# Moving a small VectorE operation behind a softmax, and three more edits to the first 20 microseconds of a fused convolution and two-layer product

## Chip, cores and metric

One core of a Trainium2 chip. The metric is the device time of one execution in microseconds (us). A run also has a span, the time from its first to its last instruction; here the time is the span plus about 1.7 us.

## The reference

```python
# x: (8, 4096, 192), weight: (8, 7), w_in: (192, 2048), w_out: (2048, 192)
w = exp(weight - max(weight)); w = w / (sum(w) + 1e-9)      # softmax over 7 taps, per head
y[b, s, h*24+d] = sum over k of w[h, k] * x_padded[b, s + k, h*24+d]   # causal, 7 taps
h = y @ w_in
g = maximum(0.01 * h, h)
out = g @ w_out                                             # (32768, 192), float32
```

## The kernel before

The sequence is cut into blocks of 512 positions of two batch rows; the first five are done as ten half blocks of 256, the rest whole. The 192 channels are three chunks of 64. For each block, VectorE (DVE) makes the seven taps of each chunk (`yt`), TensorE (PE) makes the main product with w_in into PSUM (`ph`), ScalarE (ACT) applies the leaky ReLU to it (`g`), and TensorE makes the output product with w_out (`po`). GpSimd (POOL) issues the loads of x, with a cast.

The first two half blocks (half 0 and half 1) differ: there TensorE itself makes the taps of two chunks of half 0 and of one chunk of half 1 (`acc`) with small diagonal weight matrices, each split into a high and a low bf16 part. These need a folded identity and the softmax:

```python
    load_w_in(0, 0)                                 # GpSimd: first piece of w_in
    ident = const_pool.tile([128, 128], BF16)
    make_identity(nc, ident)                        # GpSimd

    ident2 = const_pool.tile([128, CH], BF16)       # the fold, on VectorE
    nc.vector.tensor_add(ident2, ident[:, 0:CH], ident[:, CH:128])
    load_w_in(0, 1)                                 # second piece of w_in
    # ... further loads ...
    nc.vector.tensor_reduce(out=nmax, in_=w9[:, 0:K], ..., op=max, negate=True)   # softmax
    nc.scalar.activation(out=w9[:, 0:K], ..., func=Exp, bias=nmax, accum_out=...)
    # ... three bf16 parts w9p, VectorE ...
    warm(9); warm(1, 128)                           # TensorE on zeros, to raise its clock
    select(wps_hm, slice(0, 2)); warm(3); select(wps_l, 2); warm(7); warm(1, 128)
    nc.vector.tensor_copy(out=whm, in_=wps_hm)
    diag_high(0)                                    # VectorE
    cast_first(0, 0, nc.vector.tensor_copy)
    diag_low(0, range(2))                           # ScalarE
    cast_first(0, 1, nc.scalar.copy)
    transpose_first(0)
    warm(5)
    # ...
    diag_low(0, range(2, K)); diag_high(1); diag_low(1, range(K))
```

The taps on VectorE, of which the first has one tensor operand and the other six have two:

```python
                if k == 0:
                    jobs.append(lambda ...: nc.vector.tensor_scalar_mul(d, s, wk[:, c, 0:1]))
                else:
                    jobs.append(lambda ...: nc.vector.scalar_tensor_tensor(
                        out=d, in0=s, scalar=wk[:, c, k : k + 1], in1=d, op0=mult, op1=add))
```

And in the loop over groups, while the main product of the first half block runs (`u` counts its units of 12 matmuls):

```python
                if i == 0 and 2 <= u <= 5:          # half 1's taps of chunk 0 on TensorE
                    n = len(pe_ahead) // 4
                    for job in pe_ahead[(u - 2) * n : (u - 1) * n]:
                        job()
```

Of the kernel before, what the change touches and what calls it, by code (L numbers as in the profile page):

```python
# [10 lines left out]
BF16 = mybir.dt.bfloat16  # L11
# [3 lines left out]
def kernel(  # L15
# [8 lines left out]
    nc = tc.nc  # L24

    B, S, D = x.shape
    H, K = weight.shape
# [7 lines left out]
    CH = 64  # L35
# [13 lines left out]
    const_pool = ctx.enter_context(tc.tile_pool(name="const", bufs=1))  # L49
# [35 lines left out]
    def transpose_x(blk):  # L85

        if blk >= NBLK:
            return
        rp, st = divmod(blk, NB)
        if st == 0:  # L90
            new_xt(rp)
        t = x_bf.pop(blk)
        for c in range(NCH):
            nc.sync.dma_start_transpose(
                out=xt[rp][:, c, HALO + st * ST : HALO + (st + 1) * ST].rearrange(
                    "p (s k) -> p s k", s=SUB
                ),
                in_=t[:, c, :, :, :].rearrange("p s e k -> p (s e k)"),
            )
# [39 lines left out]
    def cast_first(q, e, copy):  # L139
        copy(  # L140
            out=x_half[q][:, :, :, e, :],
            in_=x_nat[q][:, e, :, :].rearrange("p s (c k) -> p c s k", c=NCH),
        )
# [3 lines left out]
    def transpose_first(q):  # L147
        ts = [
            psum_o.tile([128, HS, NCH, CH], BF16, name=f"ptr{i}", tag="po") for i in range(2)
        ]  # L150
        for s in range(HS):
            for c in range(NCH):
                for i in range(2):
                    ps = slice(i * CH, (i + 1) * CH)
                    if q != 2:
                        nc.tensor.transpose(  # L156
                            out=ts[i][:, s, c, :],
                            in_=x_half[q][ps, c, s, :, :].rearrange("p e k -> p (e k)"),
                            identity=ident[ps, ps],
                        )  # L160
                        continue
                    for e in range(2):
                        nc.tensor.transpose(  # L163
                            out=ts[i][e * CH : (e + 1) * CH, s, c, :],
                            in_=x_rows[ps, e, s, c * CH : (c + 1) * CH],
                            identity=ident[ps, ps],
                        )
        ptr[q] = ts

    def evac_first(q, *copies):  # L170
        dst = xt[0][:, :, HALO + q * HT : HALO + (q + 1) * HT].rearrange(
            "p c (i k s) -> p i s c k" if q == RUNS else "p c (s i k) -> p i s c k",
            s=HS, i=2,
        )
        for i, t in enumerate(ptr.pop(q)):
            copies[i](out=dst[:, i], in_=t)  # L176
# [4 lines left out]
    def conv_jobs(grp, chunks=range(NCH)):  # L181
        blk, t0, T = grp
        rp, st = divmod(blk, NB)
        if blk not in yt:
            yt[blk] = yt_pool.tile([128, NCH, ST], BF16, name="yt")
        y = yt[blk]
        jobs = []
        for c in chunks:
            for k in range(K):
                a = BASE + k + st * ST + t0  # L190
                src = xt[rp][:, c, a : a + T]
                dst = y[:, c, t0 : t0 + T]
                if k == 0:
                    jobs.append(
                        lambda s=src, d=dst, c=c: nc.vector.tensor_scalar_mul(  # L195
                            d, s, wk[:, c, 0:1]
                        )
                    )
                else:
                    jobs.append(  # L200
                        lambda s=src, d=dst, c=c, k=k: nc.vector.scalar_tensor_tensor(  # L201
                            out=d, in0=s, scalar=wk[:, c, k : k + 1], in1=d,
                            op0=mybir.AluOpType.mult, op1=mybir.AluOpType.add,
                        )
                    )
        return jobs
# [44 lines left out]
    def load_w_in(half, e):  # L251
        fs = slice(half * F // 2, (half + 1) * F // 2)
        nc.gpsimd.dma_start(  # L253
            out=w_in[half][e * CH : (e + 1) * CH],
            in_=moe_w_in[:, fs].rearrange("(c p) f -> p c f", p=CH),
        )

    load_w_in(0, 0)
    ident = const_pool.tile([128, 128], BF16)
    make_identity(nc, ident)  # L260

    ident2 = const_pool.tile([128, CH], BF16)
    nc.vector.tensor_add(ident2, ident[:, 0:CH], ident[:, CH:128])  # L263
    load_w_in(0, 1)
    for e in range(2):
        load_w_in(1, e)
# [14 lines left out]
    def warm(n, cols=HT):  # L281
        for _ in range(n):
            nc.tensor.matmul(  # L283
                out=wa[:, 0, 0:cols], lhsT=zero[:, 0:128], rhs=zero[:, 0:cols],
                start=True, stop=True,
            )
# [17 lines left out]
    nc.vector.tensor_sub(w9p[:, 1], w9, w9p[:, 0])  # L304
    nc.vector.tensor_sub(w9r, w9, w9p[:, 0])
    nc.vector.tensor_sub(w9p[:, 2], w9r, w9p[:, 1])
    warm(9)
    warm(1, 128)
    wps = psum_h.tile([128, 2, ST], FP32, name="wps", tag="ph")
# [17 lines left out]
    whm = const_pool.tile([128, NCH, 2, K + 1], FP32, name="whm")  # L327
# [2 lines left out]

    diag = [const_pool.tile([128, 2, K, CH], BF16, name=f"diag{c}") for c in range(NPEC)]

    def diag_high(c):
        nc.vector.tensor_mul(
            diag[c][:, 0],
            ident2[:, None, :].to_broadcast([128, K, CH]),
            whm[:, c, 0, 0:K, None].to_broadcast([128, K, CH]),
        )

    def diag_low(c, ks):  # L340
        for k in ks:
            nc.scalar.activation(  # L342
                out=diag[c][:, 1, k, :], in_=ident2,
                func=mybir.ActivationFunctionType.Copy, scale=whm[:, c, 1, k : k + 1],
            )

    diag_high(0)
    cast_first(0, 0, nc.vector.tensor_copy)
    diag_low(0, range(2))
    cast_first(0, 1, nc.scalar.copy)  # L350
    transpose_first(0)
    warm(5)
    wraw = const_pool.tile([128, NCH, K + 1], FP32, name="wraw")
    nc.vector.tensor_add(wraw, whm[:, :, 0], whm[:, :, 1])
    nc.vector.tensor_add(wraw, wps_l, wraw)
# [4 lines left out]
    nc.vector.tensor_mul(wk, wraw[:, :, 0:K], rsum.to_broadcast([128, NCH, K]))  # L360
    evac_first(0, nc.vector.tensor_copy, nc.scalar.copy)
    diag_low(0, range(2, K))
    diag_high(1)
    diag_low(1, range(K))

    def act_scale(out, in_, scale):
        nc.scalar.activation(  # L367
# [125 lines left out]
    for i, grp in enumerate(groups):  # L493
        blk, t0, T = grp
        steps = T // 64
        if t0 == 0:
            g[blk] = g_pool.tile([128, NFC, 2, ST], BF16, name="g", tag="g")
        quota = (avail - slot) // steps

        if i == 0:  # L500
            ahead = []
        else:
            ahead = conv_jobs(groups[i + 1]) if i + 1 < len(groups) else []
        per = -(-len(ahead) // steps)
        for j in range(steps):
            for u in range(2 * j, 2 * j + 2):
                mm1(grp, u)
                if i == 0 and u == 0:
                    transpose_first(1)
                    evac_first(1, nc.vector.tensor_copy, nc.vector.tensor_copy)  # L510
                    pe_ahead, evac_y = pe_conv_jobs(groups[1], 0)
                    ahead = conv_jobs(groups[1], range(1, NCH))
                    per = len(ahead)
                if i == 0 and 2 <= u <= 5:

                    n = len(pe_ahead) // 4
                    for job in pe_ahead[(u - 2) * n : (u - 1) * n]:
                        job()
                if i == 0 and u == 5:
                    evac_y(act_scale)  # L520
                if i == 0 and u == 6:
                    transpose_first(2)
            if i == 1 and j == 3:
                transpose_first(3)
            jobs = ahead[per * j : per * (j + 1)]
            if T == ST:


                jobs = ahead[len(ahead) * j // steps : len(ahead) * (j + 1) // steps]
                for job in jobs:  # L530
                    job()
                jobs = []
            for _ in range(quota):
                mm2_slot(slot)
                slot += 1
            if i == 0 and j == 3:
                evac_first(2, nc.vector.tensor_copy, nc.vector.tensor_copy)
            if i == 2 and j == 1:
                transpose_x(2)
            for job in jobs:  # L540
                job()
            if i == 1 and j == 3:
                evac_first(3, nc.vector.tensor_copy, nc.vector.tensor_copy)

            last_half = t0 + T == ST
            if j == steps // 4 and last_half:
                load_x(blk + 3)
            if j == steps // 2 and last_half and blk > 0:
                transpose_x(blk + 2)
        avail += 2 * T // 128 * NFC  # L550
# [36 lines left out]
```

## Time and profile before

| | before |
|---|---|
| time, first three runs | 694.65 us median (694.23 to 695.94) |
| span of the profiled run | 692.2 us |
| TensorE busy | 685.9 us, 99% |
| VectorE busy | 541.9 us, 78% |

The page gives busy times over the whole span and the chain of waits that ended last. The prediction below shows the lines that carried it. Instructions of before in order of time (start, length, engine, line, operation, output<-inputs, sizes, count):

```profile
113.35 4.69 DVE L201 SCALAR_TENSOR_TENSOR yt<-xt,wk,yt 128x512 bf16<-128x512 bf16 x6
...
117.71 1.49 PE L402 MATMUL ph<-yt,w_in 64*128 64x512 bf16 x12
```

VectorE's last six taps of the first whole block end at 118.04. TensorE starts that block's first product at 117.71 and, after two chunks of it, needs those taps near 118.1. Both engines arrive together; neither waits. From 14.20 to 118.04 VectorE has no idle time longer than 0.1 us.

### The profile page before, as it was taken

Reading aid. Unit: us, or ns where it says so; the run is one execution under the profiler, and the core shown is the slowest. Engines: PE = TensorE matmul, PEld = TensorE weight load, DVE = VectorE, ACT = ScalarE, POOL = GpSimd, SP = SyncE. Lnnn points to the kernel's source line nnn. Section 1 sums busy time; section 2 is a strip of 40 time slices with the busy share of each in tenths; the row PEclk is TensorE's granted clock in tenths of the full one; section 3 lists DMA queues with packets and bytes.
Section 4 is the critical chain, followed back from the end, with each engine's and each line's share of the span. In section 5 each row is a group of like instructions: output and inputs, shape, how many; then the busy total and the mean of one; then the engine's idle time right before and its main releaser. Section 6 shows DMA issues by size and latency. Waiting matters only on the chain.

```text
span 692.2 us, 26117 instructions
## 1 busy us (share of the span) xinstructions
PE 685.9 (99%) x11800; PEld 584.1 (84%) x11800; DVE 541.9 (78%) x1000; ACT 517.2 (75%) x578; POOL 144.6 (21%) x202
## 2 busy tenths in 40 slices
PE   8999999999999999999999999999999999999998
PEld 5899999788888888888888888888888888888887
DVE  5999998977878787878787878877878878787812
ACT  6888888977777777777777777777777777777771
POOL 5822211402222202222112222102222022000000
PEclk9999999999999999999999999999999999999999
DMA  9976635955565545566455565445665355322112
GB/s 175 106 90 82 92 66 78 82 82 75 66 93 81 71 78 73 71 89 86 65 78 74 78 82 85 74 75 70 83 81 79 74 74 67 70 60 59 48 42 65
DMA packets 183456, 54.00 MB, mean 78 GB/s; under 512 B 148528, under 2 KB 182576, under 8 KB 183344
## 3 DMA queue, kind: packets, MB, share of 16 engines
q0 software_dynamic: 98576, 14.56, 29.9%
q1 hardware_dynamic: 84768, 37.77, 23.6%
q8 instruction: 92, 1.51, 1.0%
q14 instruction: 20, 0.16, 0.1%
HBM read 29.88 MB, written 25.17 MB: 80 GB/s over the span
## 4 chain that ended last, share of the span: by engine, by line
PE 97%; ACT 2%; POOL 0%; DVE 0%; issue 0%; POOLq 0%
PE po L431 48%; PE ph L402 47%; ACT g L412 1%; PE acc L220 1%; PE warm L283 1%; POOL w_in L253 0%; POOL sel L242 0%; PE ptr L156 0%; PE wps L316 0%; ACT yt L367 0%; ACT w L295 0%; DVE o_sb L478 0%; PE ptr L163 0%; POOL ident masks.py:199 0%; POOL sel L240 0%
## 5 line engine op out<-in xcount | busy, mean ns | idle before, releaser
L412 ACT ACTIVATE g<-ph 128x1024 bf16<-128x1024 f32 x512 | 496.5, 1021 | 153.0 <-PE ph L402 152.6
L201 DVE SCALAR_TENSOR_TENSOR yt<-xt,wk,yt 128x512 bf16<-128x512 bf16 (+1 forms) x648 | 442.4, 683 | 17.7
L431 PEld LDWEIGHTS <-g 64*128 64x128 bf16 (+1 forms) x8064 | 360.6, 94 | 34.0 <-issue 0.2
L431 PE MATMUL po<-w_out,g 64*128 64x192 bf16 (+1 forms) x8064 | 387.3, 243 | 0.0
L402 PE MATMUL ph<-yt,w_in 64*128 64x512 bf16 (+1 forms) x3552 | 384.1, 347 | 1.2 <-ACT g L412 0.5
L402 PEld LDWEIGHTS <-w_in 64*128 64x128 bf16 x3552 | 227.3, 110 | 64.7 <-issue 4.1
L79 POOL DMA_DIRECT2D x_bf<-in_x_dram x180 | 133.9, 774 | 426.3 <-DMA xt<-x_bf 316.1
L478 DVE COPY o_sb<-po 128x192 f32<-128x192 f32 x216 | 77.1, 357 | 121.5 <-PE po L431 115.3
L195 DVE TENSOR_SCALAR yt<-xt,wk 128x512 bf16<-128x512 bf16 (+1 forms) x108 | 37.3, 345 | 1.5 <-DMA xt<-x_bf 1.4
L478 ACT COPY o_sb<-po 128x192 f32<-128x192 f32 x40 | 12.8, 321 | 2.1 <-PE po L431 0.2
L283 PE MATMUL warm<-zero 128*128 128x256 bf16 (+1 forms) x28 | 6.4, 399 | 1.1 <-DVE junk L237 1.1
L220 PE MATMUL acc<-xt,diag 64*64 64x256 bf16 x84 | 6.0, 274 | 0.0
L134 POOL DMA_DIRECT2D x_half<-in_x_dram x6 | 4.3, 716 | 6.5 <-DMA w_in<-in_moe_w_in_dram 6.5
L220 PEld LDWEIGHTS <-diag 64*64 64x64 bf16 x84 | 4.3, 107 | 1.5 <-issue 1.0
L283 PEld LDWEIGHTS <-zero 128*128 128x128 bf16 x28 | 3.4, 135 | 2.6 <-DVE junk L237 1.1
L342 ACT ACTIVATE diag<-ident,whm 128x64 bf16<-128x64 bf16 x14 | 3.6, 335 | 2.0 <-DVE whm L328 2.0
L176 DVE COPY xt<-ptr 128x384 bf16<-128x384 bf16 x7 | 2.6, 414 | 2.1 <-PE ptr L156 2.1
L253 POOL DMA_DIRECT2D w_in<-in_moe_w_in_dram x4 | 2.6, 665 | 0.0
L316 PEld LDWEIGHTS <-sel 8*64 8x64 bf16 x12 | 0.6, 139 | 1.7 <-issue 1.4
L367 ACT ACTIVATE yt<-acc,rsum 128x256 bf16<-128x256 f32 x3 | 1.4, 466 | 0.8 <-PE acc L220 0.8
L289 ACT ACT_TABLE_LOAD x1 | 1.3, 1283 | 0.8 <-PEq L571 0.8
L263 DVE TENSOR_TENSOR ident<-ident 128x64 bf16<-128x64 bf16 x1 | 0.2, 192 | 2.1 <-POOL ident masks.py:199 2.1
(37 smaller groups left out, 14.7 us busy)
## 6 DMA issues: line engine op xcount, KB each, us to landing
out_dram<-o_sb SPq DMA_DIRECT2D x118, 192.0 KB, 2.1
x_bf<-in_x_dram POOLq DMA_DIRECT2D x180, 64.0 KB, 3.3
out_dram<-o_sb SPq DMA_DIRECT2D x20, 96.0 KB, 1.6
w_in<-in_moe_w_in_dram POOLq DMA_DIRECT2D x4, 384.0 KB, 10.0
xt<-x_bf SPq DMA_TRANSPOSE x90, 2.5
w_out<-in_moe_w_out_dram POOLq DMA_DIRECT2D x1, 768.0 KB, 14.6
x_nat<-in_x_dram SPq DMA_DIRECT2D x2, 192.0 KB, 2.6
x_nat<-in_x_dram SPq DMA_DIRECT2D x1, 384.0 KB, 8.4
```

The source lines that it names most:

```text
L79: nc.gpsimd.dma_start(out=t[:, c, :, e, :], in_=src[2 * rp + e, :, :, c * CH : (c + 1) * CH],)
L134: nc.gpsimd.dma_start(out=x_half[q][:, c, :, e, :], in_=rows[:, e, :, c * CH : (c + 1) * CH],)
L176: copies[i](out=dst[:, i], in_=t)
L195: lambda s=src, d=dst, c=c: nc.vector.tensor_scalar_mul(d, s, wk[:, c, 0:1])
L201: lambda s=src, d=dst, c=c, k=k: nc.vector.scalar_tensor_tensor(out=d, in0=s, scalar=wk[:, c, k : k + 1], in1=d, op0=mybir.AluOpType.mult, ...
L220: lambda k=k, p=p, a=a, e=e, ps=ps: nc.tensor.matmul(out=acc[ps, :T], lhsT=diag[c][ps, p, k, :], rhs=xt[0][ps, c, a : a + T], start=(k == ...
L283: nc.tensor.matmul(out=wa[:, 0, 0:cols], lhsT=zero[:, 0:128], rhs=zero[:, 0:cols], start=True, stop=True,)
L342: nc.scalar.activation(out=diag[c][:, 1, k, :], in_=ident2, func=mybir.ActivationFunctionType.Copy, scale=whm[:, c, 1, k : k + 1],)
L402: nc.tensor.matmul(out=ph[:, e, i * T : (i + 1) * T], lhsT=w_in[f * 2 // NFC][ps, c, f // RUN % 2 * RUN * 128 + f % RUN : (f // RUN % 2 + ...
L412: act = nc.scalar.activation(out=g[blk][:, nf * u : nf * (u + 1), :, t0 : t0 + T], in_=ph.rearrange("p e (i t) -> p i e t", i=nf), func=my ...
L431: return nc.tensor.matmul(out=po[m], lhsT=g[b][ps, fc, e, s * 128 : (s + 1) * 128], rhs=w_out[ps, fc, :], start=start, stop=stop,)
L478: ins = copy(out=o_sb[:, n % 2, :], in_=po.pop(n))
```

## The change

Its intent is to shorten the start. The fold goes behind the softmax on VectorE, so that the softmax does not wait for GpSimd's identity. Three of the second tap set's seven low parts go from ScalarE to VectorE. Two warm-up matmuls go. Half 1's taps on TensorE come in two parts of 14 matmuls instead of four of 7.

```diff
     make_identity(nc, ident)
-
-    ident2 = const_pool.tile([128, CH], BF16)
-    nc.vector.tensor_add(ident2, ident[:, 0:CH], ident[:, CH:128])
     load_w_in(0, 1)
...
     nc.vector.tensor_sub(w9p[:, 2], w9r, w9p[:, 1])
+
+    ident2 = const_pool.tile([128, CH], BF16)
+    nc.vector.tensor_add(ident2, ident[:, 0:CH], ident[:, CH:128])
     warm(9)
...
-    def diag_high(c):
+    def diag_wide(c, p, n):
         nc.vector.tensor_mul(
-            diag[c][:, 0],
-            ident2[:, None, :].to_broadcast([128, K, CH]),
-            whm[:, c, 0, 0:K, None].to_broadcast([128, K, CH]),
+            diag[c][:, p, 0:n],
+            ident2[:, None, :].to_broadcast([128, n, CH]),
+            whm[:, c, p, 0:n, None].to_broadcast([128, n, CH]),
         )
...
-    diag_high(0)
+    diag_wide(0, 0, K)
...
-    warm(5)
+    warm(3)
...
-    diag_high(1)
-    diag_low(1, range(K))
+    diag_wide(1, 0, K)
+    diag_wide(1, 1, 3)
+    diag_low(1, range(3, K))
...
-                if i == 0 and 2 <= u <= 5:
+                if i == 0 and u in (2, 5):
 
-                    n = len(pe_ahead) // 4
-                    for job in pe_ahead[(u - 2) * n : (u - 1) * n]:
+                    n = len(pe_ahead) // 2
+                    for job in pe_ahead[(u - 2) // 3 * n : (u + 1) // 3 * n]:
                         job()
```

## The prediction

> **What bounds the kernel now.** I read the page first, then the chain of waits over the first 36 us, then the instructions in order of time over the first 30 us, and last the list of DMA completions that the trace keeps. Page:
>
> ```profile
> span 692.2 us, 26117 instructions
> PE 685.9 (99%) x11800; PEld 584.1 (84%) x11800; DVE 541.9 (78%) x1000; ACT 517.2 (75%) x578; POOL 144.6 (21%) x202
> PE   8999999999999999999999999999999999999998
> PE 97%; ACT 2%; POOL 0%; DVE 0%; issue 0%; POOLq 0%
> ```
>
> TensorE is on the path for 97% of the span. Going through the starts of its matmuls, I find only four steps longer than 0.45 us, and all lie before 24 us. Two things follow. The change touches only what is done before 24 us, so it can move the end only by what it saves there. And what it saves there reaches the end, because no later wait on a transfer is there to absorb it. The start of the chain of waits:
>
> ```profile
> 2.90 0.30 POOL ident masks.py:199
> 3.20 0.02 issue
> 3.23 0.19 DVE ident L263
> 3.42 0.07 DVE nmax L291
> ...
> 4.33 0.33 PE wps L316 x6
> 4.67 0.75 PE warm L283 x3
> 5.42 0.25 PE wps L316 x3
> 5.66 1.71 PE warm L283 x8
> 7.38 0.43 PE ptr L156 x12
> 7.81 1.18 PE warm L283 x5
> 8.99 1.74 PE acc L220 x24
> ...
> 12.75 0.48 ACT yt L367
> 13.23 0.04 issue
> 13.27 0.75 PE ph L402 x10
> ```
>
> Columns are start, length and what ran. The reader is to see that GpSimd's identity, through the small VectorE addition that folds it (L263), releases the maximum of the softmax (L291), and that everything up to 13.27 hangs on that: selection, transposes, tap products (acc), then ScalarE's scaling of the second tap product (yt). Only after that does the main product (ph) run past its first pair. In order of time:
>
> ```profile
> 3.23 0.19 DVE L263 TENSOR_TENSOR ident<-ident 128x64 bf16<-128x64 bf16 x1 [2.15 <-POOL ident masks.py:199]
> 3.33 0.14 DVE L291 TENSOR_REDUCE nmax<-w 8x1 f32<-8x7 f32 x1
> 8.25 2.97 ACT L342 ACTIVATE diag<-ident,whm 128x64 bf16<-128x64 bf16 x12
> 12.64 0.30 PE L402 MATMUL ph<-yt,w_in 64*128 64x256 bf16 x2
> 12.83 0.71 POOL L134 DMA_DIRECT2D x_half<-in_x_dram  x1 [1.73 <-DMA w_in<-in_moe_w_in_dram]
> ```
>
> The last line is the one that matters most: it is a bystander on GpSimd that waits for the second piece of w_in to land and goes at 12.83. The completions of that piece run from 9.67 to 12.54. The first main product needs this piece for its second matmul, and it went at 12.64. So the weights came in only 0.1 us before they were wanted.
>
> **What the Trainium skill says.** "TensorE: Matmul & The Clock Gate", Architectural detail: the array is 16× 32×32, says that VectorE and ScalarE queues are strict first in, first out. The trace agrees: the small weight's last completion is at 2.36, yet the reduction that needs nothing else starts at 3.33, right behind the addition. The same page, What's actually happening, says that TensorE runs at half clock until a busy window of about 3.4 us has passed, and that the window runs freely from run to run. The trace agrees: 256-column warm-up matmuls start 0.213 us apart up to 9.13, and pairs of tap matmuls of 256 columns 0.109 apart after it. "TensorEngine Tiling (Array Packing)", Key Properties, says that a change of tiling mode drains the array; here the weight loads stand still 0.20 us at each change between main product and tap product. "DMA: Bandwidth & Descriptors", Why a DMA increments its semaphore by 16 and not by 1, says only the full count means that all has landed; here the sixteenth completion comes 0.41 after the fifteenth (12.13, 12.54), so the slowest engine sets it.
>
> **The change part by part.**
>
> *The fold behind the softmax.* The reduction no longer waits for the identity. It can start at 2.36 plus the usual 0.04 of a released wait, 2.40 instead of 3.33: 0.92 us. Does someone else hold? ScalarE's first activation is over at 2.30, and the exponential would start at 2.59. TensorE's ten warm-ups let the first selection's weight load go at 3.26, and the selection would start at 4.33 − 0.92 = 3.41. So nearly all of 0.92 passes. The fold itself (0.19 us) moves into VectorE's idle 4.6 to 5.7 (now 3.7 to 4.8): free. Transposes: 7.31 → 6.39; their inputs' transfers completed at 3.79 and 4.35, so the casts move too.
>
> *Less warm-up.* Two matmuls of 0.213 go: 0.43 us. The first tap product goes from 8.92 to 8.92 − 0.92 − 0.43 = 7.57. Its input, ScalarE's copy, ends at 8.36 − 0.92 = 7.44: just in time. Sum so far 1.35.
>
> *Low parts on two engines.* Three of ScalarE's twelve scaled copies (0.238 apart) go: 0.71 us; ScalarE is free at 11.22 − 0.92 − 0.71 = 9.59. Without this it would be at 10.30, while the first tap product would end near 9.2, so it would start to hold the scaling. VectorE gets a multiplication of 192 columns; from the 448-column one (next instruction 0.53 later) I estimate 0.27. Its third-chunk taps end at 12.09 − 0.92 + 0.27 = 11.44, before they are wanted.
>
> *Where that sum goes.* Second tap product: complete at 12.72 now, then 12.72 − 1.35 = 11.37 if the clock is full by 7.57. If it turns full only at 9.13 as in this trace, 1.35 us more of taps run at half clock, which costs about 0.7: some 12.1. Scaling after it ends at 11.9 or 12.6. But the second piece of w_in comes at 12.54 whatever the compute engines do: GpSimd's issue order is untouched. So the first pair of the main product starts at about 12.60, the second at 12.71, instead of 13.27. Of 1.35 us only **0.56** is left; TensorE is expected to stand idle about a microsecond before 12.6.
>
> *Half 1's taps in two parts.* Now: four parts of 7 matmuls (3.5 pairs), each 0.55, each between main products of 0.78, hence 1.33 per unit. After: two parts of 14, each 7 × 0.109 + 0.11 = 0.87, so 0.46 less in all, and main products that follow another cost 0.655 instead of 0.78. Against that, with less TensorE work between them, units wait for ScalarE's 1.02 per unit. Counting from the start of the third unit: third 0 to 0.78, taps to 1.65, fourth to 2.31, fifth to 2.97; the sixth needs the bank that ScalarE frees at 3.54, so 3.58 to 4.36, taps to 5.24, seventh at 5.24. It is now at 20.45 − 15.12 = 5.33. Gain **0.09**; TensorE's saved work is mostly turned into one wait of 0.6.
>
> Sum on one clock phase: 0.56 + 0.09 = 0.65 us, 0.1% of the time.
>
> *The clock's phase.* Today TensorE has a hole of 1.0 us at 3.3 to 4.3, so a full busy window can begin only at 4.33 and the clock turns full, by the phase, somewhere in 7.7 to 11.2; every microsecond of that after 8.92 costs about half a microsecond. This would explain part of the spread of before (693.86 in the profiled run, 694.23 to 695.94 in the others). After, the hole shrinks to 0.15, so the clock should turn full up to 3.4 us sooner (5.7 on this trace's phase), and any remainder hides behind w_in. That is worth another 0 to 0.8 against the median.
>
> **The rivals.** (1) The whole 1.35 us shows, because w_in lands earlier than I think or the wait isn't binding: second pair at 11.9, time about 692.9. Against it: completion at 12.54 in the trace and a bystander that waited for it. (2) Nothing shows: w_in lands later than in this trace, since its slowest engine varies. 0.5 us later would eat the gain: 694.5. (3) The idle microsecond before the main product sends the clock back to half: up to 3.4 us at half speed costs 1.7, time about 695.3. Against it: today's hole of 1.0 us before 4.33 only delayed the rise, and I know no fall in this trace. (4) The two-part taps make ScalarE the bound: if its backlog is 0.3 longer than I count, the gain of 0.09 becomes a loss of 0.2, time about 693.8.
>
> **Range and chances.** 693.86 − 0.65 = 693.2 from the profiled run, 694.65 − 0.65 = 694.0 from the median; I take 693.6. The spread of before, 1.7 us, is larger than the effect, so the range is 692.5 to 694.9. Two per cent is 13.9 us, ten times all that the first 13 us could give; faster or slower by that much would need something quite unforeseen: within 2% at 0.98, 0.01 on each side.
>
> **What would show it.** Reduction at 2.4; first selection at 3.4; first tap product near 7.5; the main product's second matmul held until the second piece of w_in, near 12.6, with TensorE idle before it; the seventh unit 5.2 after the third; from there on starts earlier by 0.6 to 0.7 and unchanged steps of 2.63 per main product and output product. Full-clock spacing before 9 us would confirm the phase argument. If the main product starts before 12.3, the cap was wrong; if it starts at 12.6 and the end is still not earlier, something after 24 us absorbed it.

## The result, and the profile after

Ratios here and below are the mean time of one kernel's fast runs over that of the other's of the same rounds, so they are not quite the ratio of the medians quoted.

| | before | changed |
|---|---|---|
| time, first rounds (4 runs each) | 695.23 us median (694.23 to 695.94) | 693.18 us median (692.82 to 693.83) |
| ratio, first rounds | | 0.9973 (95%: 0.9955 to 0.9990) |
| ratio, later rounds (9 and 5 runs) | | 0.9986 (0.9973 to 0.9998) |
| span of the profiled run | 692.2 us | 692.1 us |

The change is 0.95 to 1.9 us faster by the mean, and within 2% by far. But the two profiled executions differ by only 0.1 us, so the traces say at once that something took a gain back in the one that was profiled. The start of the changed kernel, in order of time:

```profile
2.17 0.15 DVE L288 TENSOR_REDUCE nmax<-w 8x1 f32<-8x7 f32 x1 [1.10 <-DMA w<-in_weight_dram]
...
3.26 0.33 PE L316 MATMUL wps<-w9p,sel 8*64 8x16 bf16 x6
...
4.53 1.01 PE L280 MATMUL warm<-zero 128*128 128x256 bf16 x8
...
6.40 0.50 PE L280 MATMUL warm<-zero 128*128 128x256 bf16 x3
...
7.25 1.72 PE L220 MATMUL acc<-xt,diag 64*64 64x256 bf16 x28 [0.35 <-ACT diag L342]
...
11.68 0.84 PE L403 MATMUL ph<-yt,w_in 64*128 64x256 bf16 x11 [0.50 <-DMA w_in<-in_moe_w_in_dram]
...
12.71 1.06 DVE L176 COPY xt<-ptr 128x384 bf16<-128x384 bf16 x2 [1.40 <-PE ptr L156]
```

The reduction starts at 2.17 instead of 3.33, the tap product at 7.25 instead of 8.92, and the main product goes on at 11.68, when the second piece of w_in has landed, instead of 13.27. The eight warm-ups from 4.53 take 1.01 us where the same eight took 1.78 from 5.60 before: the clock turned full at 4.60 in the trace's clock record, against 9.13. VectorE starts its unbroken run of copies and taps at 12.71 instead of 14.20. So far 1.5 us are won. The place where half blocks give way to whole blocks, near 118 us: I call it **the switch**. The switch in the changed kernel:

```profile
113.33 4.69 DVE L201 SCALAR_TENSOR_TENSOR yt<-xt,wk,yt 128x512 bf16<-128x512 bf16 x6
...
116.18 0.63 PE L403 MATMUL ph<-yt,w_in 64*128 64x512 bf16 x4
...
118.08 1.06 PE L403 MATMUL ph<-yt,w_in 64*128 64x512 bf16 x8 [1.27 <-DVE yt L201]
```

TensorE comes at 116.18, 1.53 us earlier than before, and then stands still until 118.08 for VectorE. VectorE's last taps start at 113.33, against 113.35: it has lost all its lead. The page's chain of waits had turned accordingly:

```profile
PE 82%; DVE 14%; DMA 1%; ACT 1%; issue 1%; POOL 0%; POOLq 0%
```

VectorE was under 1% of this chain before, and TensorE 97%. Where did VectorE's lead go? All first taps of the two kernels from 12 to 119 us (duration in ns: least, median, longest), before and then changed:

```profile
L195 DVE TENSOR_SCALAR yt<-xt,wk x29: 280/281/349, 15.3 to 113.0; 128x256 bf16<-128x256 bf16 x26, 128x512 bf16<-128x512 bf16 x3
```

```profile
L195 DVE TENSOR_SCALAR yt<-xt,wk x30: 277/282/668, 13.8 to 118.5; 128x256 bf16<-128x256 bf16 x26, 128x512 bf16<-128x512 bf16 x4
```

The median is the same, but the longest went from 0.35 us, the ordinary length at 512 columns, to 0.67, at 256 columns. Six first taps of the changed kernel are stretched, by 1.47 us together; in before one is, by 0.02. An example from the changed kernel:

```profile
58.97 2.24 POOL L79 DMA_DIRECT2D x_bf<-in_x_dram  x3 [12.39 <-issue]
59.21 1.94 ACT L413 ACTIVATE g<-ph 128x1024 bf16<-128x1024 f32 x2 [0.29 <-PE ph L403]
59.21 0.53 DVE L195 TENSOR_SCALAR yt<-xt,wk 128x256 bf16<-128x256 bf16 x1
```

GpSimd had begun to issue a load of x at 58.97; the first tap began at 59.21, took 0.53 instead of 0.28, and the next tap could start only after it. The Trainium skill, "SBUF — State Buffer", Who interferes with whom, says that VectorE's one-tensor operations can use a port pair that is shared with GpSimd, and that whoever issues first holds it while the other blocks. The traces agree in part, as told at the end.

### The profile page after: what moved, and what is told of

Its sections match the earlier page's. It is cut to its first block, busy times and chain, and to the rows that moved or that the text cites. A ratio compares the mean times of both kernels' runs of the same rounds, so it can differ in the third digit from the quotient of the medians.

```text
span 692.1 us, 26111 instructions
## 1 busy us (share of the span) xinstructions
PE 684.0 (99%) x11798; PEld 584.3 (84%) x11798; DVE 543.6 (79%) x1001; ACT 516.6 (75%) x575; POOL 144.6 (21%) x202
## 4 chain that ended last, share of the span: by engine, by line
PE 82%; DVE 14%; DMA 1%; ACT 1%; issue 1%; POOL 0%; POOLq 0%
PE po L432 42%; PE ph L403 40%; DVE yt L201 13%; DMA w_in<-in_moe_w_in_dram 1%; DVE yt L195 1%; ACT g L413 1%; DVE xt L176 0%; POOL w_in L253 0%; POOL sel L242 0%; DVE o_sb L479 0%; POOL sel L240 0%; PE ptr L156 0%; POOL ident masks.py:199 0%; POOL ident masks.py:197 0%; POOLq masks.py:199 0%
## 5 line engine op out<-in xcount | busy, mean ns | idle before, releaser
L280 PE MATMUL warm<-zero 128*128 128x256 bf16 (+1 forms) x26 | 4.9, 340 | 1.1 <-DVE junk L237 1.1
L140 ACT CAST x_half<-x_nat 128x384 bf16<-128x384 f32 x3 | 1.5, 503 | 0.3 <-DMA x_nat<-in_x_dram 0.3
```

What stands on the lines that cost most here:

```text
L280: nc.tensor.matmul(out=wa[:, 0, 0:cols], lhsT=zero[:, 0:128], rhs=zero[:, 0:cols], start=True, stop=True,)
```

## The experiments

Three theories were set down before the runs. **V**: the gain of the start must pass through VectorE's unbroken chain of taps, which ends at the switch. **P**, the prediction's: TensorE alone sets the pace, and what it saves early reaches the end. **C**: the phase of TensorE's clock alone makes the difference. The expectation of the fourth run extended V by the stretching, and the sum below stood in that of the fifth, so before three of the seven traces in its table were taken.

**The account that all traces share.** In every trace in which VectorE neither idles before the switch nor has other work, three numbers read from the trace add up: the start of its chain (the first copy `xt<-ptr` of half 1), the stretching (first taps over 0.281 us at 256 columns or 0.347 at 512, summed), and the end of the taps of the first whole block.

| kernel | second w_in piece landed | chain starts | chain ends | length | stretch | length less stretch | span less end |
|---|---|---|---|---|---|---|---|
| before | 12.54 | 14.20 | 118.04 | 103.84 | 0.02 | 103.82 | 574.11 |
| changed | 11.63 | 12.71 | 118.03 | 105.32 | 1.47 | 103.85 | 574.06 |
| fold only | 12.12 | 13.20 | 118.47 | 105.27 | 1.44 | 103.83 | 574.04 |
| all but the fold | 12.21 | 14.16 | 119.20 | 105.04 | 1.23 | 103.81 | 574.07 |
| changed, again | 11.82 | 12.90 | 117.25 | 104.35 | 0.51 | 103.84 | 574.04 |
| more TensorE work | 11.92 | 13.00 | 118.15 | 105.15 | 1.33 | 103.82 | 574.05 |
| w_in first | 10.38 | 15.88 | 120.39 | 104.51 | 0.68 | 103.83 | 574.07 |

Chain start + 103.8 + stretch + 574.1 gives the span to 0.1 us in all seven. TensorE's saving in the first 24 us doesn't appear in it at all, except through the start of the chain. That start in turn follows the landing of w_in: in all nine traces with the fold behind the softmax and the old order of issue it comes 1.08 or 1.09 us after it.

### The fold alone

```diff
-    ident2 = const_pool.tile([128, CH], BF16)                          # before the softmax
-    nc.vector.tensor_add(ident2, ident[:, 0:CH], ident[:, CH:128])
...
     nc.vector.tensor_sub(w9p[:, 2], w9r, w9p[:, 1])
+    ident2 = const_pool.tile([128, CH], BF16)
+    nc.vector.tensor_add(ident2, ident[:, 0:CH], ident[:, CH:128])
```

> The kernel before with one part of the change alone: the fold of the identity moved behind the softmax. Theory V (the prologue's gain must pass through VectorE's unbroken chain of taps, which ends at the switch from half to whole blocks near 118 us, and is there as large as the lead that chain still has): reduction at 2.2 to 2.4, clock full before 6 us, VectorE's chain starts 0.9 to 1.5 us earlier than the 14.20 of before because w_in caps it, and the time is 0.5 to 2 us under before, ratio 0.997 to 0.9993, most of what the whole change gives. Theory P (the prediction's: the end moves by what TensorE saves before 24 us): 0.5 to 0.9 us under before. Theory C (the clock's phase alone makes the measured 2 us): the clock turns as early as in the changed kernel, so the ratio is that of the whole change, 0.997.

Measured: 694.23 us median (693.65 to 695.59), before in the same rounds 695.01; ratio 0.9993 (0.9979 to 1.0006), which the interval leaves unclear. By the means it is 0.53 us faster, at the lower edge of what V and P both expected. The trace is clearer:

```profile
6.43 0.72 PE L280 MATMUL warm<-zero 128*128 128x256 bf16 x5
...
7.23 1.72 PE L220 MATMUL acc<-xt,diag 64*64 64x256 bf16 x28
...
12.16 0.74 PE L402 MATMUL ph<-yt,w_in 64*128 64x256 bf16 x10 [1.00 <-DMA w_in<-in_moe_w_in_dram]
```

With five warm-ups and all low parts on ScalarE, the tap product starts at 7.23, as in the changed kernel at 7.25, and the main product waits for w_in just the same. In the trace the fold is thus the whole gain of the start; the rest of the change shortens nothing that is waited for. The profiled run lost 1.44 us to stretching. Theory C as I wrote it expected 0.997 here, which lies outside the interval, by a little; the whole change's later ratio, 0.9986, lies inside, so this doesn't settle C.

### All of it but the fold

```diff
     make_identity(nc, ident)
+    ident2 = const_pool.tile([128, CH], BF16)
+    nc.vector.tensor_add(ident2, ident[:, 0:CH], ident[:, CH:128])
...
-    ident2 = const_pool.tile([128, CH], BF16)                          # behind the softmax
-    nc.vector.tensor_add(ident2, ident[:, 0:CH], ident[:, CH:128])
```

> The changed kernel with the fold put back in front of the softmax, all other parts kept. Reduction again near 3.3, TensorE's hole of 1 us back. Theory V and P: first tap product 0.43 us earlier than before (two warm-ups less), main product some 0.3 to 0.5 us earlier, time 0.2 to 0.6 us under before. Theory C: clock turns as late as before, so the time is that of before, ratio 1.000 within 0.0007.

Measured: 694.87 us median (694.11 to 695.95), ratio 1.0000 (0.9985 to 1.0015). The tap product started 0.44 earlier (8.48), but the clock was not yet full, and it took 2.20 instead of 1.81:

```profile
8.48 2.20 PE L220 MATMUL acc<-xt,diag 64*64 64x256 bf16 x28
```

So the two warm-ups taken away came back as slower taps, and the chain started at 14.16. My expectation of 0.2 to 0.6 us (V and P) was missed by the mean, though the interval, 1 us to each side, would allow it; the trace shows its error, which was to count warm-ups as pure cost while the clock was still half. Theory C's number, 1.000, was met. This run therefore doesn't tell C from V as the table has it: in both the late clock leaves the start where it was. What speaks against C as the whole cause is that the clock enters the table only through the start of the chain, and that the stretching, all of it seen while the clock was full, moves the span as much.

### Relieving VectorE with ScalarE, first try, on the changed kernel and on before

```diff
-                if k == 0:
+                if k == 0 and c == 2 and 0 < blk < NHALF:
+                    jobs.insert(0, lambda ...: nc.scalar.activation(
+                        out=d, in_=s, func=Copy, scale=wk[:, c, 0:1]))
+                elif k == 0:
```

> The changed kernel, with the first tap of the third chunk of the eight half blocks from 2 to 9 made on ScalarE instead of VectorE: 2.5 us less work in VectorE's chain up to the switch near 118 us, 8 times some 0.4 us more on ScalarE, TensorE's work unchanged. Theory V: TensorE's wait of 1.3 us for VectorE at the switch is gone, the switch comes 1 to 1.6 us earlier than in the changed kernel's profile, and the time is 0.4 to 1.5 us under the changed kernel: ratio to before 0.995 to 0.9967. Theory P: TensorE's lead already reached the end, ratio stays at 0.9973 (0.9968 to 0.9978). If ScalarE becomes the bound: slower.

> The kernel before with the same relief of VectorE, nothing else. In the profile of before VectorE and TensorE reach the switch at the same time to 0.1 us. Theory V with collisions (GpSimd's DMA issues stretch some of VectorE's first taps, by chance 0 to 1.5 us a run): the spread of before shrinks and its slow runs (695.8, 695.9) go; mean 0.5 to 1.2 us under before, ratio 0.9983 to 0.9993. Theory C (the spread of before is the clock's phase in the prologue): relief does not touch it, ratio 0.9997 to 1.0003 and the same spread.

Measured on the changed kernel: 693.26 us median (692.76 to 693.89), ratio to before 0.9977 (0.9965 to 0.9990): V's number (0.995 to 0.9967) was missed and P's (0.9968 to 0.9978) met. On before: 694.46 (693.95 to 695.07), 0.9994 (0.9981 to 1.0007); the spread was 1.1 us against 2.0 of before in the same rounds, but five runs against nine do not settle a spread, and 0.9994 lies between V's and C's numbers. The waits of VectorE up to the switch on the changed kernel say why little was won:

```profile
DVE yt L209 <- ACT yt L196: 1.8, 3, 0.8
```

The edit took 2.5 us of work from VectorE and gave it 1.8 us of waiting for ScalarE's taps, in half blocks 7 to 9, where VectorE is ahead. The test was badly placed and tells the theories apart poorly; it was mended below.

### The changed kernel again, more VectorE work, more TensorE work

The second was meant to lengthen VectorE's chain by two operations into a spare tile, the third to lengthen TensorE's by eight pairs done twice in half block 6:

```diff
+                    if blk == 3 and c == 0 and k == 1:
+                        jobs.append(lambda ...: nc.vector.scalar_tensor_tensor(
+                            out=spare, in0=s, scalar=wk[:, c, 0:1], in1=s, op0=mult, op1=add))
```

```diff
+            again = blk == 3 and t0 == 0 and u < 4
-            for c in range(NCH):
+            for c in [-1] * again + list(range(NCH)):
+                extra, c = c < 0, max(c, 0)
...
-                        stop=(c == NCH - 1),
+                        stop=(c == NCH - 1) or extra,
```

> The changed kernel once more, for a second trace on the same chip and session as the next three. Theory V: whatever its time, the span is the end of VectorE's taps of the first whole block plus 574.0 us, and that end is the start of its chain (about 12.7 to 13.2) plus 103.85 us plus what its first taps were stretched by GpSimd's DMA issues, unless TensorE comes later. Time 692.8 to 694, ratio to before 0.9968 to 0.998.

> The changed kernel with two more tap operations of 256 columns on VectorE in half blocks 6 and 7, into a spare tile (results right): 2 x 0.52 = 1.04 us more in VectorE's chain, nothing on TensorE. Theory V: the time grows by nearly all of it, 0.7 to 1.05 us over the changed kernel of the same rounds. Theory P (TensorE sets the pace before the switch): VectorE's extra microsecond hides in its slack, 0 to 0.2 us.

> The changed kernel with eight pairs of main-product matmuls of half block 6 done twice (the second overwrites the first, results right): 8 x 0.109 = 0.87 us more on TensorE, nothing on VectorE. Theory V: hides in TensorE's wait at the switch wherever that is over 0.9 us (1.3 in the profile), time 0 to 0.4 us over the changed kernel. Theory P: 0.8 to 0.9 us over it.

Measured medians: 693.57 (693.01 to 694.88), 694.63 (693.72 to 694.72) and 694.06 (693.63 to 694.76). The changed kernel again fits V's account (the table), with a stretch of 0.51 and a span of 691.3 us; its ratio, 0.9986, missed the expected 0.9968 to 0.998. More VectorE work: by means 0.69 us over the changed kernel, just under V's range, but inconclusive: the trace shows that the extra operation waited for nothing and ran in the tail of the tap before it (its chain, less stretch, is 0.24 us longer instead of 1.04). More TensorE work, whose 0.87 us do show in TensorE's arrival at the switch:

```profile
117.34 0.63 PE L405 MATMUL ph<-yt,w_in 64*128 64x512 bf16 x4
...
118.20 1.06 PE L405 MATMUL ph<-yt,w_in 64*128 64x512 bf16 x8 [0.23 <-DVE yt L201]
```

TensorE came at 117.34 and still waited for VectorE, so in this run the 0.87 us cost nothing. By the means of five runs it cost 0.48 us, between the two theories' numbers. That fits V where a run has little stretching, as in the run of the changed kernel just told, whose TensorE waited only 0.31 us at the switch; it is not proof of it.

### First taps in the two-operand form

```diff
-                        lambda ...: nc.vector.tensor_scalar_mul(d, s, wk[:, c, 0:1])
+                        lambda ...: nc.vector.scalar_tensor_tensor(
+                            out=d, in0=s, scalar=wk[:, c, 0:1], in1=s, op0=mult, op1=bypass)
+                        if blk <= NHALF
+                        else nc.vector.tensor_scalar_mul(d, s, wk[:, c, 0:1])
```

> The changed kernel with the first tap of each chunk, up to the first whole block, written as the two-operand form that the other taps have and that no trace showed stretched: 26 taps of 256 columns at 0.522 instead of 0.317 apart and 3 of 512 at 0.785 instead of 0.38, so 6.5 us more of VectorE, and no stretching. Theory V with collisions: no first tap is longer than 0.50 (256 columns) or 0.77 (512); the chain takes 103.85 + 6.5 us; TensorE waits some 7 us at the switch; time 5 to 5.6 us over the changed kernel (6.5 less the 0.9 to 1.5 of stretching that goes), and the spread among its runs is that of the start of the chain alone, under 0.8 us. If the stretching comes from something other than the operation's form, stretched taps are still seen and the time is 6.3 us or more over. Theory P: VectorE's slack hides part, under 3 us.

Measured: 700.73 us median (700.31 to 701.59), 7.1 over the changed kernel by the means, where 5 to 5.6 was expected. This is over the 6.3 us that I had set as a sign against the form as the cause, but the trace says otherwise: five first taps started 0.18 to 0.36 us after GpSimd began an issue, where the other form is stretched, and no first tap is longer than its work. The form does decide the stretching:

```profile
L195 DVE SCALAR_TENSOR_TENSOR yt<-xt,wk x29: 479/480/747, 14.7 to 118.3; 128x256 bf16<-128x256 bf16 x26, 128x512 bf16<-128x512 bf16 x3
```

(480 ns is 256 columns, 747 is 512.) The chain ran from 13.56 to 123.76, 110.2 us, against 103.85 + 6.5 = 110.35 expected. P, which expected VectorE's slack to hide part of it, is out. The missing 2 us lie around the switch (columns: stretch, busy time and count of PE, PEld, DVE, ACT, POOL, then the granted clock):

```profile
110.00:116.00 6.00, 6.00 (x132) 6.00 (x128) 5.79 (x8) 5.09 (x8) 0.00 (x0) 1.00 0.11 36
118.00:123.50 5.50, 0.77 (x8) 0.17 (x4) 5.29 (x8) 0.47 (x2) 0.90 (x2) 0.80 0.34 58
123.80:128.00 4.20, 4.19 (x30) 2.52 (x31) 4.02 (x6) 2.05 (x2) 3.26 (x5) 0.50 1.20 76
129.00:135.00 6.00, 5.93 (x82) 4.11 (x79) 5.72 (x9) 5.82 (x9) 0.00 (x0) 1.00 0.55 78
```

TensorE waited about 5 us for VectorE, its clock fell to half, and it worked at 0.50 until 128.11. The span ended 576.1 us after the end of the chain, where 574.05 is the rule. This wait was paid twice; waits of 1.27 us (changed) and 2.93 us (the last run below) at the same place left the clock full.

### A better placed relief, w_in first, both, and a chained test of VectorE

The relief keeps ScalarE's taps to half blocks 2 to 6 and the first whole block:

```diff
+    ACT_TAPS = {(1, 0), (1, HT), (2, 0), (2, HT), (3, 0), (NHALF, 0)}
...
-                if k == 0:
+                if k == 0 and c == 2 and (blk, t0) in ACT_TAPS:
+                    jobs.insert(0, lambda ...: nc.scalar.activation(...))   # as above
+                elif k == 0:
```

> The changed kernel with a better placed relief: ScalarE makes the first tap of the third chunk in half blocks 2 to 6 and in the first whole block only, 5 x 0.317 + 0.38 = 2.0 us less in VectorE's chain, in places where VectorE isn't ahead of ScalarE. Theory V: no idle of VectorE before the switch, TensorE's wait there under 0.2 us, span near TensorE's own 690.6 to 690.9, mean 0.7 to 1.3 us under the changed kernel's pooled mean: ratio to before 0.9963 to 0.9975; spread small. Theory P: ratio as of the changed kernel, 0.998.

Measured: 692.96 us median (692.07 to 693.41), before 695.72 in the same rounds; ratio **0.9961** (0.9948 to 0.9974). The waits from 110 to 125 us no longer hold one of TensorE for VectorE, and at the switch TensorE runs through:

```profile
116.96 1.49 PE L412 MATMUL ph<-yt,w_in 64*128 64x512 bf16 x12
```

VectorE's taps ended at 116.68, before TensorE came. This run had 1.38 us of stretching and the relief absorbed it; its w_in landed late (12.41), which now sets the time: TensorE came to the switch 104.55 us after that landing, as in both traces of the changed kernel. It beats before clearly, by slightly more than V expected (0.9963 to 0.9975), and P's 0.998 lies outside the interval. That it beats the changed kernel is what the ratios (0.9961 against 0.9973 and 0.9986) point to, but it is not shown: the two were not run in the same rounds, their intervals overlap, and its traced span, 691.7 us, lies between the changed kernel's two (692.1 and 691.3).

```diff
+    load_w_in(0, 0)
+    load_w_in(0, 1)
     sel = const_pool.tile([H, NCH, CH], BF16, name="sel")      # GpSimd, for the selection
...
-    load_w_in(0, 0)
     ident = const_pool.tile([128, 128], BF16)
     make_identity(nc, ident)
-    load_w_in(0, 1)
```

> The changed kernel with the first two pieces of w_in issued ahead of the selection mask and the identity on GpSimd, so the second piece is asked for 1.5 us sooner. If its landing caps the start of the main product (11.6 to 12.5 in nine traces): it lands 0.4 to 1 us sooner, the main product's second matmul moves as far, down to some 11.5 where ScalarE's scaled taps come next, VectorE's chain starts at 12.4 to 12.6, and the time falls 0.3 to 0.6 us below the changed kernel's: ratio 0.9970 to 0.9977. If the cap is something else, no change: 0.998.

> Both of the two edits above together on the changed kernel. Under theory V and the cap they add: TensorE reaches the switch near 116.0 and VectorE is there before it, span 690.2 to 690.5, ratio to before 0.9955 to 0.9968, spread under 0.8 us. If VectorE still comes last, the second edit alone shows, 0.9965 to 0.9975.

Measured: 696.68 us median (696.16 to 697.47), ratio 1.0018 (1.0006 to 1.0030); with the relief 695.68 (695.04 to 695.95), 1.0002. Both expectations were clearly missed. The second piece of w_in did land sooner, at 10.38. Two other things moved:

```profile
3.84 0.33 PE L317 MATMUL wps<-w9p,sel 8*64 8x16 bf16 x6 [0.51 <-POOL sel L254]
...
7.11 0.51 ACT L140 CAST x_half<-x_nat 128x384 bf16<-128x384 f32 x1 [1.07 <-DMA x_nat<-in_x_dram]
...
8.86 3.19 PE L220 MATMUL acc<-xt,diag 64*64 64x256 bf16 x28
```

The selection waited for its mask. The second piece of x for the first half block, issued at 1.74 as ever, landed at 7.09 instead of about 4.35, behind w_in in the transfer engines. TensorE therefore had holes, its clock turned full only at 12.84, and the first tap product took 3.19 us instead of 1.72. So the cap by w_in could not be lifted by this order of issue; that the two loads compete for the same early bandwidth is how I read the two landings (1.8 us sooner than 12.14, the mean of the twelve traces with the old order; 2.7 us later), and was not tested by itself.

The chained test of VectorE, the mend of the inconclusive one:

```diff
+                    if blk == 3 and c < 2 and k == 4:
+                        jobs.append(lambda ...: nc.vector.scalar_tensor_tensor(
+                            out=spare, in0=s, scalar=wk[:, c, 0:1], in1=d, op0=mult, op1=add))
```

> The earlier test of a longer VectorE chain, mended: two extra operations did not wait for the tap before them and hid in its tail (0.24 us added instead of 1.04). Here four extra ones of 256 columns in half blocks 6 and 7 read the tap result before them, 0.44 to 0.52 us each, 1.8 to 2.1 us in all, TensorE unchanged. Theory V: TensorE's wait at the switch grows to 2.5 to 3.5 us and the time by 1.6 to 2.1 us over the changed kernel (pooled ratio 0.998): 1.0003 to 1.001. Theory P: under 0.4 us more, 0.9985 at most.

Measured: 696.64 us median (695.29 to 697.36), ratio 1.0014 (1.0001 to 1.0026). At the switch:

```profile
117.45 0.63 PE L411 MATMUL ph<-yt,w_in 64*128 64x512 bf16 x4
...
121.01 1.06 PE L411 MATMUL ph<-yt,w_in 64*128 64x512 bf16 x8 [2.93 <-DVE yt L209]
```

The chain took 120.95 − 13.32 − 1.74 (stretch) = 105.89 us, 2.05 more than 103.84, as much as was added, and the span was again the end of the chain plus 574.05. The time rose by about 0.34% against the changed kernel's 0.998 (of other rounds), some 2.4 us, which is above V's 1.0003 to 1.001; this run's stretch of 1.74 us is the largest of all. In the trace the work added to VectorE before the switch shows in full. P, which allowed 0.9985 at most, is refuted, and V's account of the trace holds.

## Why the prediction was right or wrong

The predicted time (693.6) and range (692.5 to 694.9) held, and the class did. The steps did not all hold. That the number came out was in part luck: the gain at the start was sized too small, and it was wrongly passed on in full to the end.

- **The fold, 0.92 us: right.** The reduction moved by 1.16, because its weight had landed at 2.15 in this trace, against 2.36 in that of before, and the selection by 1.07, from where TensorE's own warm-ups set it (3.26).
- **Less warm-up, 0.43 us: wrong.** The tap product starts at 7.25 with three warm-ups and at 7.23 with five. Once the clock is full a warm-up costs half, and TensorE waits for the copies of x in both cases. While the clock is half, as in the kernel without the fold, fewer warm-ups only give slower taps.
- **Low parts on two engines: right that it hides.** ScalarE scaled the first tap product at 9.04 instead of 9.81 with the fold alone; the main product waits for w_in either way.
- **The cap by the second piece of w_in: right, its size wrong.** The term I sized at 0.56 took the landing at 12.54 from the one trace of before. In the twelve traces with the same order of issue it landed between 11.63 and 12.54, so that trace was the latest of all. In the profiled run the main product went on at 11.68 instead of 13.27. In the eight traces whose start is that of the changed kernel, VectorE's chain began between 12.71 and 13.56, so 0.6 to 1.5 us, on average 1.0 us, before the 14.20 of before.
- **Half 1's taps in two parts, 0.09 us: about right and without effect.** Third to seventh unit took 5.29 instead of 5.33 us. VectorE's chain does not pass through it.
- **"What it saves there reaches the end, because no later wait on a transfer is there to absorb it": this step failed.** I looked for later waits on transfers and for holes of TensorE, found none, and did not look at how little room the engine that feeds it had. VectorE's chain had none: it reached the switch in the same 0.1 us as TensorE. The output product began 1.53 us earlier (22.63 instead of 24.16), and in the profiled run all of it became a wait at the switch. By V's account what passes is the earlier start of VectorE's chain, 0.6 to 1.5 us, less the difference in stretching; by the means of the two sets of rounds 0.95 and 1.9 us did pass.
- **The clock's phase: right that the clock turns full sooner.** It did so at 4.60 to 6.76 in all nine traces with the fold behind the softmax and GpSimd's order as it was, against 9.13 in before. As a cause of before's spread it is not shown: the changed kernel's runs spread by 1.0 and 1.9 us too, and stretching ranged from 0.02 to 1.74 us. Assuming V's account, the mean spans of before in the three later sets of rounds, 693.0 to 693.7 us, and a chain start of 14.2 give an average stretch of 0.9 to 1.6 us: an estimate, and it would make before's profiled run a lucky one.

By the same account, the profile of before looked as if TensorE alone were on the path because that execution happened to have almost no stretching.

Open: how the gain divides among the parts in time and not only in the trace (fold alone 0.9993 and whole change 0.9973 or 0.9986 overlap), and why the alignment of GpSimd's issues with first taps falls out as it does in a run.

## What to carry to other kernels

A chain of waits that names one engine for 97% does not say that the others have room: before you count an early gain, find where that engine next takes data from an engine without idle time, and compare the two arrival times there. If they are within your expected gain, the second engine's chain is what you must shorten, and one execution's trace may show it at its luckiest, so take a second trace. A wait of TensorE of some 5 us cost clock as well as time.

## What the Trainium skill lacked or had wrong

- "SBUF — State Buffer", Who interferes with whom: it says who blocks, not what GpSimd's issuing of one load costs VectorE. In these traces an issue of 0.71 to 0.89 us cost a one-tensor operation of 0.28 us between 0 and 0.47 us. A first tap that started 0.2 to 0.5 us after an issue's start did not end before 0.74 to 0.94 us after it; one that started less than 0.18 us after it lost under 0.01 us, and one that started later than 0.5 at most 0.11. The page has the holder block the other for its whole instruction; the recorded issue blocked only in its middle, by these numbers. The sum over some 29 first taps was 0.02 to 1.74 us from run to run.
- "TensorE: Matmul & The Clock Gate", What's actually happening: it speaks of a busy window but not of how much idle time one may hold. Here, a hole of 1.0 us near 3.3 us (before) went with a full clock at 9.13; no hole there with 4.60 to 6.76 (nine traces); two holes of 0.51 and 0.80 us (w_in first) with 12.84. That the holes were the cause is not shown.
- In no page: the spread of landing times. A piece of w_in issued at 3.14 landed between 11.63 and 12.54 in twelve runs.
